# Cos and sin from PSUM, bands in halves, a plain first visit and zero matmuls in a convolution and wave-mixing kernel

## The chip, the cores and the metric

The kernel runs on one core of a Trainium2 chip. The metric is the time of one execution on the device in microseconds (us); of several runs the median is given. A profile is the record of one execution. The engines are named as in the profile: PE is TensorE (matmuls), PEld its weight loads, DVE is VectorE, ACT is ScalarE, POOL is GpSimd and SP is SyncE, which here only issues DMAs.

## The reference

`x` has 8 batches, 4224 tokens and 192 channels. First a causal convolution over 7 tokens runs in each of 8 heads (24 channels each) with softmaxed taps. Its output, again called x, goes through a wave layer. The large part is the mixing over tokens with two 4224 x 4224 matrices.

```python
w = softmax(weight)                       # 8 heads x 7 taps
x = einsum('hk,bskhg->bshg', w, windows_of_7(x))
theta = x @ w_theta                       # 192 x 192
zr, zi = x * cos(theta), x * sin(theta)
y = einsum('ts,bsd->btd', w_tok_r, zr) + einsum('ts,bsd->btd', w_tok_i, zi)
u = x + y
out = u + maximum(u @ w_ch, 0)
```

All inputs and the output are float32. The kernel multiplies in bfloat16 and accumulates in float32.

## The kernel before, in words

**Tiling.** The columns of the token mixing are batch and channel together, 8 x 192 = 1536, split in two halves `g` of 768 (`HN`), each again in two of 384 (`PC`), one PSUM bank per product. Input tokens form 33 chunks of 128, each made of four quarters of 32 tokens from different places of the sequence. Output tokens form 17 units: sixteen pairs of 128-row tiles and a single one. A visit works on one unit with the chunks that are at hand, at most 11 (`SLOTS`). The first visit has chunks 0 and 1, and each of the next nine adds one chunk. Later, chunk c takes the slot of chunk c - 11. After a visit the partial sums of its unit go to DRAM and come back at the unit's next visit.

**Seven products instead of eight.** For a pair of row tiles, the weights of both matrices are a 2 x 2 block A, and the data zr, zi in two halves a 2 x 2 block B. The kernel uses seven products in the manner of Strassen and Winograd (L766 to L846): sums S1 to S4 of the weight blocks (`total`, L576) and T1 to T4 of the data blocks (`sum`, L450). One product costs one 128x384 matmul for each chunk and each half, at L721. With two chunks the first visit has 28 of them.

**A chunk's preparation.** A window loads three quarters of x with halo rows (L277, L293); eight matmuls with the bands, a banded matrix of taps for each head, do the convolution (L323); copies bring the result from PSUM to `xz` (L185 on ScalarE, L183 on VectorE). TensorE transposes it through `ident` (L494), copies bring it to `uT`, and the theta product follows (`channel_mix`, L509). VectorE clamps the angles to +-1.5 on their way from PSUM to the float32 tile `ang` (L397). ScalarE takes cosine and sine of `ang`, 768 columns at a time, into the slot's z tiles r0, i0, r1 (t1 for late chunks) and i1 (L425). VectorE multiplies them by x (L434) and makes the T sums (L446).

**Weights of a visit.** DMAs on POOL's queue load blocks of the two token matrices as bfloat16 into `st` (L542); VectorE transposes them in 32 x 32 blocks (L564) and makes the S sums (L578). Results leave PSUM by adding them into the float32 tiles `d` (L745), or by a plain copy where a unit begins.

**Order.** All steps after the start are planned when the program is built. A `Step` has an engine, a length in us, the steps it follows, and sometimes a bank. `Schedule` walks a model time forward; each engine, when free, takes the ready step with the earliest due time, and the order so found is the order of the instructions on each engine. `START` says when engines and the first data are free. Convolutions, transposes and theta products share banks 6 and 7 (`mm`); the first ones borrow banks 2 to 5 (`lent`). Products use banks 0 to 5: x in 0 and 1, y in 2 and 3, s in 4 and 5. In-order engines mean that an instruction that waits holds up all that stand behind it on its engine.

**The start.** TensorE runs 24 warm-up matmuls on zeros (L963). POOL makes the 0/1 masks with seven selects (L902), a 0/1 `block` with six (L911), and loads `w_theta` (L225). VectorE makes the softmax (L917 to L928), `taps` as a sum of masks (L934), `terms` = taps times weights for all heads (L939), the sum over the 7 taps in three steps (L948) and the three parts of the bands (L953). Before the first visit, two matmuls with `ident` fill the y banks (L781).

Of the kernel before, what the change touches and what calls it, by code (L numbers as in the profile page):

```python
# [16 lines left out]
def kernel(  # L17
# [43 lines left out]
    CLAMP = 1.5  # L61
    EXTRA = 3
    BY_PE = 4
    EITHER, TURNED = 4, 11
# [89 lines left out]
    def parts(u):  # L154
        return 14 if pair(u) else 8
# [58 lines left out]
    nc.vector.memset(bands[:, :, WQ, :], 0.0)  # L214

    def channel_weights(w, name, after=None):
        R = D - P
        made = {}

        def clear():  # L220
            made["t"] = t = wk.tile([P, 4, D], BF16, name=name, tag="wc", bufs=1)
            nc.vector.memset(t[:, 1:3, :], 0.0)

        def load(lo, hi, k, r0, r1):
            pool(nc.gpsimd.dma_start(out=made["t"][lo:hi, k, :], in_=w[r0:r1, :]))  # L225

        pieces = ((0, P, 0, 0, P), (0, R, 1, P, D), (R, P, 2, 0, R), (0, P, 3, R, D))
        if after is None:
            clear()
            for p in pieces:  # L230
                load(*p)
            ready = [Step("none", 0.0, None)]
            ready[0].fixed = START["wth"]
        else:
            ready = [Step("pool", 0.25, lambda: (clear(), load(*pieces[0])), after, lands=4.0, wire=0.3)]
            for p in pieces[1:]:
                ready.append(Step(
                    "pool", 0.6, lambda p=p: load(*p), ready[:1], lands=4.0, wire=0.3
                ))
        return (lambda: made["t"]), ready  # L240

    xw = tiles(wk, 3, [P, B, D], BF16, "xw", bufs=3)
    rings = {k: Ring(2) for k in ("uT", "ang", "xr", "st", "x", "y", "s")}
# [9 lines left out]
    class Window:  # L253
        def __init__(self):
            self.m = len(windows)
            windows.append(self)
            self.k, self.uses, prev = rings["xw"].take()
            self.loads = []
            self.rows = []
            for j in range(WQ):  # L260
                t0, lo = tokens(*divmod(self.m * WQ + j, NQ)), j * ROWS + KS - 1
                s = self.load(lo, t0, Q, prev)
                self.rows.append(s)
                self.loads.append(s)
            for j in range(WQ):
                t0, lo = tokens(*divmod(self.m * WQ + j, NQ)) - KS + 1, j * ROWS
                if t0 < 0:
                    nc.vector.memset(xw[self.k][0 : KS - 1, :, :], 0.0)
                elif self.m < 2:
                    self.loads.append(self.load(lo, t0, KS - 1, prev))  # L270
                else:
                    self.loads.append(self.halo(j, lo, prev))
# [88 lines left out]
    class Chunk:  # L361
# [5 lines left out]
        def prepare(self):  # L367
# [10 lines left out]
            self.ang, angles, anguse, self.z, self.t = {}, {}, {}, {}, {}  # L378
            for g in range(2):
# [6 lines left out]
                ak, anguse[g], prev = rings["ang"].take()  # L386
                self.ang[g] = angt[ak]
                for k2 in range(2):
                    m = Step(
                        "pe", 0.34, lambda b, k2=k2, uT=uT: channel_mix(b, uT, k2, wth()),  # L390
                        [turned, wth_ready, prev], mm=True,
# [4 lines left out]
                    e = Step(  # L396
                        "dve", 0.55, lambda b, k2=k2, g=g: dve(nc.vector.tensor_scalar(  # L397
                            out=self.ang[g][:, k2 * 2 * D : (k2 + 1) * 2 * D],
                            in0=banks[b][:, 0 : 2 * D],
                            scalar1=-CLAMP, scalar2=CLAMP, op0=ALU.max, op1=ALU.min,  # L400
                        )), [m], frees=m,
                    )
                    anguse[g].append(e)
                angles[g] = [s for s in anguse[g]]
            slot = c % SLOTS

            def take(name, key, steps_after, engine, us, run):

                prev = zuses[slot].get(name, [])
                s = Step(engine, us, run, [steps_after, prev])  # L410
                zuses[slot][name] = [s]
                return s

            self.ready = {}
            names = {(0, 0): "r0", (1, 0): "i0", (0, 1): "r1" if self.early else "t1", (1, 1): "i1"}
# [3 lines left out]

            for i, g in ((0, 0), (1, 0), (0, 1), (1, 1)):  # L420
                name = names[i, g]
                self.z[i, g] = z = ztiles[slot][name]

                def wave(z=z, i=i, g=g):
                    act(nc.scalar.activation(  # L425
                        out=z, in_=self.ang[g], func=AT.Sin,
                        **({"bias": half_pi[:], "scale": 1.0} if i == 0 else {}),
                    ))

                w = take(name, None, angles[g], "act", 0.93 if i == 0 else 0.84, wave)  # L430
                anguse[g].append(w)

                def times(z=z, g=g):
                    dve(nc.vector.tensor_tensor(  # L434
                        out=z, in0=self.xf[:, g * HN : (g + 1) * HN], in1=z, op=ALU.mult
                    ))

                s = Step("dve", 0.58, times, [w])
                use(name, s)
                self.xzuse.append(s)  # L440
                self.ready["B" + str(i + 1) + str(g + 1)] = s
            B = self.ready
            self.where = {"B11": "r0", "B21": "i0", "B22": "i1", "T2": "t2", "T4": "t4"}
# [6 lines left out]
            def sum(name, o, p, q, after):  # L450

                if o in (p, q):
                    s = Step("dve", 0.58, minus(o, p, q), after)
                    use(o, s)
                else:
                    s = take(o, None, after, "dve", 0.58, minus(o, p, q))
# [66 lines left out]
    class Weights:  # L523
        def __init__(self, v):
# [70 lines left out]
            turn("A12", "A12")  # L595
            total("S3", "A11", "A21", ALU.subtract, r["A11"] + r["A21"])
# [64 lines left out]
    class Visit:  # L661
# [104 lines left out]
        def products(self):  # L766
# [4 lines left out]
            for r in "xys" if self.pair else "xy":  # L771
                for g in gs:
                    k, uses[r, g], prev[r, g] = rings[r].take()
                    rows[r, g] = 2 * "xys".index(r) + k
                    if self.v == 0 and r != "x":
# [3 lines left out]
                        if r == "y":  # L779
# [32 lines left out]

            for g in gs:
# [34 lines left out]
        def output(self, q):  # L848
            k, use, prev = outring.take()
            if len(outring.uses) <= 5:  # L850
                prev = [
                    s for r in ("ang", "xz", "uT", "xw") for u in rings[r].uses[-3:] for s in u
# [37 lines left out]
    START = {"x": (8.0, 11.0), "pe": 11.3, "dve": 11.3, "act": 6.3, "pool": 11.2, "sp": 2.0, "wth": 15.0}  # L890
# [4 lines left out]
    EARLY, SLACK, CALM = {}, 12.0, 30.0  # L895
    noise = wk.tile([P, 512], BF16, name="noise", tag="ang")
    nc.vector.memset(noise, 0.0)
    Window()
    masks = wk.tile([WR, KS, WQ, Q], BF16, name="masks", tag="ang")
    nc.gpsimd.memset(masks, 1.0)  # L900
    for k in range(KS):
        nc.gpsimd.affine_select(  # L902
            out=masks[:, k, :, :], in_=masks[:, k, :, :], pattern=[[ROWS, WQ], [1, Q]],
            channel_multiplier=-1, base=k, compare_op=ALU.is_equal, fill=0.0,
        )
    Window()
    block = constp.tile([WR, WQ], F32, name="block")
    nc.gpsimd.memset(block, 1.0)
    for j in range(WQ):
        for sign, base in ((1, -j * ROWS), (-1, (j + 1) * ROWS - 1)):  # L910
            nc.gpsimd.affine_select(  # L911
                out=block[:, j : j + 1], in_=block[:, j : j + 1], pattern=[[0, 1]],
                channel_multiplier=sign, base=base, compare_op=ALU.is_ge, fill=0.0,
            )
    wth, wth_ready = channel_weights(moe_w_theta, "wth")
# [6 lines left out]
    nc.scalar.activation(out=wsb, in_=wsb, func=AT.Exp)  # L922
    nc.scalar.activation(out=wmax[:, 0:1], in_=wsb[:, 0, 0:1], func=AT.Sin)
    nc.vector.tensor_reduce(out=wsum, in_=wsb, axis=mybir.AxisListType.X, op=ALU.add)
# [7 lines left out]
    taps = wk.tile([WR, KS, Q], BF16, name="taps", tag="xz", bufs=3)  # L932
    for j in range(1, WQ):
        nc.vector.tensor_tensor(  # L934
            out=taps, in0=masks[:, :, 0, :] if j == 1 else taps, in1=masks[:, :, j, :],
            op=ALU.add,
        )
    terms = spool.tile([WR, KS, H, Q], BF16, name="terms", tag="st")
    nc.vector.tensor_tensor(  # L939
        out=terms, in0=taps[:, :, :].unsqueeze(2).to_broadcast([WR, KS, H, Q]),  # L940
        in1=wbf[0:WR, :, :].rearrange("p h k -> p k h").unsqueeze(3).to_broadcast(
            [WR, KS, H, Q]
        ), op=ALU.mult,
    )
    n = KS
    while n > 1:
        k = n // 2
        nc.vector.tensor_tensor(  # L948
            out=terms[:, 0:k], in0=terms[:, 0:k], in1=terms[:, n - k : n], op=ALU.add
        )  # L950
        n -= k
    for j in range(WQ):
        nc.vector.tensor_scalar_mul(  # L953
            out=bands[:, :, j::NQ, :],
            in0=terms[:, 0].unsqueeze(2).to_broadcast([WR, H, 2, Q]),
            scalar1=block[:, j : j + 1],
        )
    ident = constp.tile([P, P], BF16, name="ident")
    make_identity(nc, ident)

    for k in range(6):
        for _ in range(4):
# [3 lines left out]
    angt = tiles(wk, 2, [P, HN], F32, "ang")  # L966
# [14 lines left out]
    for i, v in enumerate(sequence):  # L981
        for c in entering.get(v, []):
            convolved(c).prepare()
        if v == settled:
# [10 lines left out]
        at += (hi - lo) * parts(u) * (PC / 2400 + 0.0025)  # L995
# [130 lines left out]


# [36 lines left out]
```

## Time and profile before

| | |
|---|---|
| median of 5 runs | 1430.98 us (1426.12 to 1437.35) |
| the profiled execution | 1426.12 us, span 1424.4 us |
| busy: PE, DVE, ACT, POOL | 1398.6, 1100.1, 429.6, 510.3 us |
| mean granted clock of TensorE | 0.993 |
| products at L721 | 7572 matmuls |
| theta and output matmuls at L509, convolution at L323 | 192 columns each; 352 at L323 |
| HBM read, written | 248.53 MB, 104.99 MB |

The span runs from the first instruction to the last. Busy times are those of the profile; matmuls are pipelined, so a busy TensorE is not one at its peak, and counting matmuls in a stretch says more. In rows by group the columns are: line, engine, operation, output<-input with shapes, count, then busy time and the mean of one in ns, then the idle time of the engine just before and what ended it. A row of a timeline begins with the start and the duration in us.

### The profile page before, as it was taken

The page shows a single profiled execution, that of the slowest core. Times are in us where ns is not written, and L with a number is a line of the kernel's source. Part 1 is how long each engine was busy: PE and PEld are TensorE (multiplying, and loading weights), DVE is VectorE, ACT ScalarE, POOL GpSimd, SP SyncE. Part 2 cuts the span into 40 slices and gives each one's busy share as a digit, 9 for nine tenths or more (in the row PEclk, how much of TensorE's full clock was granted, in tenths as well). Part 3 has the DMA queues.
Part 4 walks back from the last instruction along what each step waited for, and adds up shares of the span by engine and source line. Part 5 has one row for each costly group of instructions (what it writes and reads, how often), then busy time and mean ns, then how long its engine had stood idle before and what let it go on. Part 6 is the DMA issues. An engine that isn't in the chain of part 4 may idle for free.

```text
span 1424.4 us, 24789 instructions
## 1 busy us (share of the span) xinstructions
PE 1398.6 (98%) x9318; PEld 884.3 (62%) x9318; DVE 1100.1 (77%) x1803; ACT 429.6 (30%) x761; POOL 510.3 (36%) x779
## 2 busy tenths in 40 slices
PE   6899999999999999999999999999999999999998
PEld 4566666666666666666666666666666666666665
DVE  7998855454887987877657699788897888887787
ACT  5886532212522332320000333234231212111232
POOL 8533321212423464125113445523546153432120
PEclk7999999999999999999999999999999999999999
DMA  8999884567999999999678999999997999999994
GB/s 105 205 228 192 167 161 111 110 116 148 256 207 215 238 232 245 221 216 188 197 166 197 236 223 246 235 238 213 223 220 180 230 257 247 270 238 206 195 257 145
DMA packets 335776, 291.27 MB, mean 204 GB/s; under 512 B 157524, under 2 KB 284500, under 8 KB 335656
## 3 DMA queue, kind: packets, MB, share of 16 engines
q0 software_dynamic: 169232, 97.75, 50.6%
q1 hardware_dynamic: 126424, 182.09, 42.0%
q10 hardware_dynamic: 40000, 9.84, 4.9%
q8 instruction: 73, 1.20, 0.3%
q14 instruction: 47, 0.39, 0.1%
HBM read 248.53 MB, written 104.99 MB: 248 GB/s over the span
## 4 chain that ended last, share of the span: by engine, by line
PE 92%; DVE 3%; issue 1%; DMA 1%; POOL 1%; ACT 1%; SPq 0%; DVEq 0%; POOLq 0%; ACTq 0%
PE bank L721 84%; PE bank L509 5%; PE bank L323 2%; DMA st<-in_moe_w_tok_i_dram 1%; PE bank L494 1%; DVE d L745 1%; DVE w L564 1%; POOL xw L277 1%; DVE d L874 1%; DVE ang L397 0%; ACT xz L185 0%; DVE w L578 0%; DMA xw<-in_x_dram 0%; DVE r L434 0%; ACT r L425 0%
## 5 line engine op out<-in xcount | busy, mean ns | idle before, releaser
L721 PEld LDWEIGHTS <-w 128*128 128x128 bf16 x7572 | 734.8, 98 | 461.3 <-issue 7.9
L721 PE MATMUL bank<-t,w 128*128 128x384 bf16 x3198 | 562.0, 326 | 2.2 <-DVE w L578 0.9
L745 DVE TENSOR_TENSOR d<-bank,d 128x384 f32<-128x384 f32 x532 | 286.9, 547 | 171.7 <-PE bank L721 142.8
L564 DVE STREAM_TRANSPOSE w<-st 128x640 bf16<-128x640 bf16 (+4 forms) x412 | 342.5, 854 | 68.3 <-PE bank L721 55.4
L721 PE MATMUL bank<-r,w 128*128 128x384 bf16 x2154 | 392.1, 326 | 1.4 <-DVE r L434 0.8
L721 PE MATMUL bank<-i,w 128*128 128x384 bf16 x2220 | 389.1, 326 | 1.6 <-DVE bank L183 1.3
L542 POOL DMA_DIRECT2D st<-in_moe_w_tok_r_dram x240 | 137.6, 582 | 400.1 <-DVE w L564 385.6
L542 POOL DMA_DIRECT2D st<-in_moe_w_tok_i_dram x240 | 136.9, 579 | 167.2 <-DVE w L564 150.2
L578 DVE TENSOR_TENSOR w<-w 128x1408 bf16<-128x1408 bf16 (+9 forms) x216 | 182.0, 843 | 2.4
L185 ACT ACTIVATE xz<-bank 32x384 bf16<-32x384 f32 (+2 forms) x300 | 139.7, 481 | 99.3 <-issue 58.4
L277 POOL DMA_DIRECT2D xw<-in_x_dram x137 | 79.1, 584 | 194.5 <-PE bank L323 149.9
L693 POOL TENSOR_TENSOR d<-d,xr 128x768 f32<-128x768 f32 x61 | 103.3, 1695 | 81.6 <-DMA xr<-xs 35.4
L425 ACT ACTIVATE r<-ang,half_pi 128x768 bf16<-128x768 f32 x44 | 41.0, 933 | 285.3 <-DVE ang L397 285.1
L185 ACT ACTIVATE bank<-bank 128x384 f32<-128x384 f32 x111 | 52.3, 474 | 210.6 <-PE bank L721 189.3
L185 ACT ACTIVATE d<-bank 128x384 f32<-128x384 f32 x126 | 60.8, 490 | 137.0 <-PE bank L721 136.2
L397 DVE TENSOR_SCALAR ang<-bank 128x384 f32<-128x384 f32 x132 | 70.7, 552 | 35.9 <-PE bank L509 35.2
L855 ACT ACTIVATE ubT<-d 128x768 bf16<-128x768 f32 x43 | 36.2, 842 | 143.1 <-DVE d L745 131.9
L509 PEld LDWEIGHTS <-uT 128*128 128x128 bf16 x632 | 56.9, 100 | 18.7 <-issue 3.5
L874 DVE SCALAR_TENSOR_TENSOR d<-bank,d 128x384 f32<-128x384 f32 x106 | 54.4, 546 | 12.5 <-PE bank L509 10.8
L509 PE MATMUL bank<-wth,uT 128*128 128x192 bf16 x528 | 62.2, 253 | 0.8 <-ACT uT L185 0.3
L323 PE MATMUL bank<-xw,bands 114*128 114x192 bf16 x352 | 53.2, 252 | 8.3 <-DVE bands L953 4.8
L425 ACT ACTIVATE i<-ang 128x768 bf16<-128x768 f32 x66 | 54.7, 829 | 8.1 <-PE bank L721 8.1
(76 smaller groups left out, 553.9 us busy)
## 6 DMA issues: line engine op xcount, KB each, us to landing
part<-d SPq DMA_DIRECT2D x168, 384.0 KB
d<-part SPq DMA_DIRECT2D x155, 384.0 KB
st<-in_moe_w_tok_r_dram POOLq DMA_DIRECT2D x156, 176.0 KB, 6.2
st<-in_moe_w_tok_i_dram POOLq DMA_DIRECT2D x156, 176.0 KB, 7.1
out_dram<-d SPq DMA_DIRECT2D x53, 384.0 KB
xw<-in_x_dram POOLq DMA_DIRECT2D x132, 96.0 KB, 4.7
xs<-xz SPq DMA_DIRECT2D x132, 96.0 KB
xr<-xs POOLq DMA_DIRECT2D x66, 192.0 KB, 6.3
```

What stands on the lines that cost most here:

```text
L185: act(nc.scalar.activation(out=o(), in_=i(*b), func=AT.Copy))
L277: pool(nc.gpsimd.dma_start(out=xw[self.k][lo : lo + n, :, :], in_=x[:, t0 : t0 + n, :].rearrange("b s d -> s b d"),))
L323: pe(nc.tensor.matmul(banks[b][:, hh * B * G : (hh + 1) * B * G], lhsT=bands[:, h, at : at + NQ, :].rearrange("p z m -> p (z m)"), rhs=xw[ ...
L397: "dve", 0.55, lambda b, k2=k2, g=g: dve(nc.vector.tensor_scalar(out=self.ang[g][:, k2 * 2 * D : (k2 + 1) * 2 * D], in0=banks[b][:, 0 : 2 ...
L425: act(nc.scalar.activation(out=z, in_=self.ang[g], func=AT.Sin, **({"bias": half_pi[:], "scale": 1.0} if i == 0 else {}),))
L509: pe(nc.tensor.matmul(banks[bk][:, b * D : (b + 1) * D], lhsT=tT[:, 3 * k + b + i, :], rhs=w[:, 2 * b + i, :], start=(i == 0), stop=(i == ...
L542: "pool", 0.58, lambda a=a, t0=t0, i=i, w=w: pool(nc.gpsimd.dma_start(out=st[i][a * Q : (a + 1) * Q, 0:nb, 0 : n * Q], in_=w[r0 : r0 + nb ...
L564: lambda c=c, ce=ce: dve(nc.vector.transpose(self.tile(name)[:, c:ce, :, :], st[i][:, at : at + NQ, c * Q : ce * Q].rearrange("p bt (c j) ...
L578: s = Step("dve", 0.15 + 0.069 * n, lambda: dve(nc.vector.tensor_tensor(out=flat(self.tile(name)), in0=flat(self.tile(p)), in1=flat(self.t ...
L693: a = Step("pool", 1.75, lambda: pool(nc.gpsimd.tensor_tensor(out=tile_(), in0=tile_(), in1=xrt[k], op=ALU.add)), [r, s])
L721: pe(nc.tensor.matmul(banks[bank][:, 0:PC], lhsT=self.w.block(a, c), rhs=chunks[c].operand(b, g), start=(start and c == self.lo), stop=(c ...
L745: dve(nc.vector.tensor_tensor(out=o, in0=y, in1=o, op=ALU.add))
```

## The change

- The clamp and the `ang` tiles are gone. ScalarE takes cosine and sine straight from the PSUM bank of the theta product, 384 columns at a time, into the z tile. So the theta product is followed by two ScalarE steps that free its bank, and it now waits for the former users of both z tiles of its half.
- The first visit (`v < PLAIN`, with `PLAIN = 1`) uses eight plain products and needs no S or T sums. Four rings of banks x, y, s and x once more (`z`) take its results, each written out once. The T sums of chunks 0 and 1 are made at visit 1, and the two matmuls at L781 are gone.
- The bands are made in two halves of four heads; one of the three parts of each half is written by ScalarE. The masks come from one select over all taps, on a tile set to one by VectorE; `block` is a maximum over masks on VectorE.
- `w_theta` comes as float32 over SP's queue and is converted by ScalarE. The halo loads of the first two windows stand behind the select and `make_identity`. There are 18 warm-up matmuls. `START` is changed.
- While model time is below `WARM = 60`, the planner emits a 128x128 matmul of zeros wherever its TensorE is free, and counts 0.11 us for it. It adds zeros to columns 384 to 511 of bank 0, which no product uses.

```diff
+            for g in range(2):
...
+                waves = {0: [], 1: []}
+                places = [zuses[slot].get(names[i, g], []) for i in waves]
                 for k2 in range(2):
                     m = Step(
                         "pe", 0.34, lambda b, k2=k2, uT=uT: channel_mix(b, uT, k2, wth()),
-                        [turned, wth_ready, prev], mm=True,
+                        [turned, wth_ready, places], mm=True,
                     )
-                    e = Step(
-                        "dve", 0.55, lambda b, k2=k2, g=g: dve(nc.vector.tensor_scalar(
-                            out=self.ang[g][:, k2 * 2 * D : (k2 + 1) * 2 * D],
-                            in0=banks[b][:, 0 : 2 * D],
-                            scalar1=-CLAMP, scalar2=CLAMP, op0=ALU.max, op1=ALU.min,
-                        )), [m], frees=m,
-                    )
+                    for i in waves:
+                        def wave(b, z=ztiles[slot][names[i, g]], i=i, cols=cols):
+                            act(nc.scalar.activation(
+                                out=z[:, cols], in_=banks[b][:, 0 : 2 * D], func=AT.Sin,
+                                **({"bias": half_pi[:], "scale": 1.0} if i == 0 else {}),
+                            ))
+                        w = Step("act", 0.5, wave, [m], frees=m)
...
+            if v < PLAIN:
+                return
             total("S3", "A11", "A21", ALU.subtract, r["A11"] + r["A21"])
...
+            if self.v < PLAIN:
+                for g in gs:
+                    k, uses["z", g], prev["z", g] = rings["x"].take()
+                    rows["z", g] = k
+                for r, i, j in (("x", 1, 1), ("y", 1, 2), ("s", 2, 1), ("z", 2, 2)):
+                    for g in gs:
+                        product(r, g, f"A{i}1", f"B1{j}", start=True)
+                        product(r, g, f"A{i}2", f"B2{j}")
+                        add(2 * i + j - 3, r, g, begins=True, ends=True)
+                return
...
-    START = {"x": (8.0, 11.0), "pe": 11.3, "dve": 11.3, "act": 6.3, "pool": 11.2, "sp": 2.0, "wth": 15.0}
+    START = {"x": (7.5, 10.5), "pe": 7.5, "dve": 10.5, "act": 8.3, "pool": 8.3, "sp": 4.5, "wth": 9.0}
...
+    for lo, hi, k, r0, r1 in pieces:
+        sp(nc.sync.dma_start(out=wth_f[lo:hi, k, :], in_=moe_w_theta[r0:r1, :]))
     Window()
+    nc.gpsimd.affine_select(
+        out=masks, in_=masks, pattern=[[1, KS], [ROWS, WQ], [1, Q]],
+        channel_multiplier=-1, base=0, compare_op=ALU.is_equal, fill=0.0,
+    )
+    windows[0].halos()
     Window()
+    make_identity(nc, ident)
+    windows[1].halos()
...
+    for hs in (slice(0, H // 2), slice(H // 2, H)):
         nc.vector.tensor_tensor(
+            out=terms[:, :, hs], in0=taps[:, :, :].unsqueeze(2).to_broadcast([WR, KS, H // 2, Q]),
...
+        for j in (1, 0, 2):
+            o = bands[:, hs, j::NQ, :]
+            i = terms[:, 0, hs].unsqueeze(2).to_broadcast([WR, H // 2, 2, Q])
+            if j == 1:
+                nc.scalar.activation(out=o, in_=i, func=AT.Copy, scale=block[:, j : j + 1])
+            else:
+                nc.vector.tensor_scalar_mul(out=o, in0=i, scalar1=block[:, j : j + 1])
...
+        for c in range(NCH):
+            if max(enter[c], PLAIN) == v:
+                chunks[c].sums()
...
+            if now < WARM and self.free["pe"] <= now + 1e-9:
+                self.free["pe"] = now + 0.11
+                if self.emit:
+                    pe(nc.tensor.matmul(
+                        banks[0][:, 3 * P : 4 * P], lhsT=noise[:, 0:P], rhs=noise[:, 0:P],
+                        start=False, stop=True, skip_group_check=True,
+                    ))
```

## Prediction

> **What bounds the kernel now.** I read the page first, then the chain of waits for the price of a steady product, then the busy times by stretch, and last the timeline of the first 45 us.
>
> ```profile
> PE 1398.6 (98%) x9318; PEld 884.3 (62%) x9318; DVE 1100.1 (77%) x1803; ACT 429.6 (30%) x761; POOL 510.3 (36%) x779
> ...
> PEclk7999999999999999999999999999999999999999
> ```
>
> TensorE is busy for 98% of the span and its clock is whole except at the very start. The chain of waits has a stretch with nothing else in it:
>
> ```profile
> 185.82 160.22 PE bank L721 x986
> ```
>
> So a 128x384 product costs 160.22/986 = 0.1625 us. In the same way the timeline's runs at full clock give 0.082 us for a 192-column matmul and 0.056 for a 128-column transpose. With these prices I counted the matmuls in each stretch (groups by shape). From 100 to 1400 us they fill the time: 0.3 us too much or too little in most hundreds, in all about 2 us lost. From 1400 to the end 9.9 us are lost. In the first 100 us 35.9 are lost: 10.0, 7.0, 6.9, 4.4, 3.7, 1.3 in the first six tens, then 1.7 and 0.9 in the two twenties. **So the bulk of what can be won lies before 100 us.** The stretches show who is late there (columns: length, busy time of PE, PEld, DVE, ACT, POOL, clock, DMA share, GB/s):
>
> ```profile
> 10.00:20.00 10.00, 6.04 (x40) 5.18 (x41) 6.94 (x15) 3.61 (x7) 9.99 (x25) 0.58 0.79 100
> 20.00:30.00 10.00, 6.96 (x40) 4.32 (x39) 8.63 (x21) 7.57 (x13) 9.01 (x17) 0.67 1.39 164
> 30.00:40.00 10.00, 7.47 (x48) 4.57 (x47) 9.36 (x19) 8.50 (x15) 2.40 (x5) 0.90 0.42 47
> 40.00:50.00 10.00, 7.93 (x57) 4.58 (x55) 9.64 (x23) 9.07 (x17) 6.26 (x11) 1.00 1.25 237
> 50.00:60.00 10.00, 9.06 (x73) 5.92 (x70) 9.61 (x20) 8.84 (x18) 3.98 (x7) 1.00 1.21 238
> 60.00:80.00 20.00, 19.26 (x134) 11.63 (x133) 18.76 (x38) 17.55 (x35) 10.29 (x18) 1.00 1.20 231
> 80.00:100.00 20.00, 19.44 (x153) 13.06 (x151) 17.44 (x33) 15.35 (x31) 9.44 (x17) 1.00 1.07 209
> ```
>
> From 20 to 80 us VectorE and ScalarE are both full; TensorE waits for them. Before 20 us it waits for the bands, and later for chunk 1:
>
> ```profile
> 13.22 2.74 PE L323 MATMUL bank<-xw,bands 114*128 114x192 bf16 x16 [4.84 <-DVE bands L953]
> ...
> 25.04 0.85 PE L323 MATMUL bank<-xw,bands 114*128 114x192 bf16 x4 [2.06 <-ACT xz L185]
> ...
> 33.48 0.48 PE L721 MATMUL bank<-r,w 128*128 128x384 bf16 x2 [0.85 <-DVE r L434]
> ```
>
> The clock falls twice, at about 11.6 and 25.2 us:
>
> ```profile
> 15.00:18.40 3.40, 2.67 (x21) 2.00 (x19) 2.70 (x5) 2.25 (x6) 3.40 (x7) 0.50 0.96 121
> 18.40:21.80 3.40, 3.07 (x18) 2.36 (x17) 2.61 (x6) 2.01 (x3) 3.34 (x6) 0.50 1.49 165
> 21.80:25.20 3.40, 1.24 (x9) 0.70 (x9) 3.30 (x8) 3.37 (x7) 3.11 (x6) 1.00 1.27 143
> ```
>
> **Bands in two halves, and the start.** In the trace wbf is ready at 5.71, the terms take 2.02 us, their sums 1.35, the three band writes 1.03, and the last band is done at 13.16. Now a maximum over 672 mask columns stands ahead of wbf; 2.02 us for 1792 columns and 0.21 for 56 put it at about 0.85. So wbf comes at 6.7, the first half (1.0 + 0.86 + 0.5) at 9.1 and the second at 11.5. POOL loses two memsets, thirteen selects and four weight loads and gains one long select (seven of 96 columns took 1.63; I put it at 1.0), so its first weight load for the visits goes from 13.49 to about 9.3. The w_theta loads on SP stand ahead of that queue's first other job at 6.26, and hide. But chunk 0 also needs window 1, whose last issue moves only from about 10 to 9.3; with 3.2 us to land (the median) its convolutions can start at 12.5, not at about 14.6. Two cases. If the clock holds, the first product comes at about 18.5 instead of 22.16 (3.7 earlier). If not, the zero matmuls placed between the two windows (the planner thinks window 0 done at 8.4 and window 1 due at 10.7: 2.3/0.11 = 21 of them) run in front of window 1 at half clock, 21 x 0.11 = 2.3 us, and 1.9 are won. I take the middle, **-2.8**.
>
> Here the Trainium skill (TensorE: Matmul & The Clock Gate, Part 1) says that one idle window of some 3.4 us halves the clock and one busy window restores it. The fall at 11.6, 3.2 us after the last warm-up matmul, fits. The return does not: matmuls resumed at 13.22, were 79% busy from 15.0 to 18.4, and the clock came back only at 21.8, after 8.6 us. By the page, a drop in the thin stretch from 7 to 11.6 would be over by about 15; by the row it could last until 22, and of the 2.8 us hardly 1 would stay. The fillers are plain matmuls and close up; I side with the page and keep the row for the range.
>
> **First visit with plain products.** It removes four S sums (0.28 each), and replaces 14 evictions and copies by 8 (0.49 to 0.55 each): 1.1 + 6 x 0.52 = 4.2 us of VectorE and ScalarE work. The eight T sums of chunks 0 and 1 (0.55 each) are moved behind the first visit, not removed. With both engines full, half of the 4.2 is time: **-2.1**. It adds four products, **+0.65**, of TensorE, which is idle there; once TensorE is the bound this counts in full.
>
> **Cos and sin from PSUM.** The relevant rows:
>
> ```profile
> L425 ACT ACTIVATE r<-ang,half_pi 128x768 bf16<-128x768 f32 x44 | 41.0, 933 | 285.3 <-DVE ang L397 285.1
> L185 ACT ACTIVATE bank<-bank 128x384 f32<-128x384 f32 x111 | 52.3, 474 | 210.6 <-PE bank L721 189.3
> L185 ACT ACTIVATE d<-bank 128x384 f32<-128x384 f32 x126 | 60.8, 490 | 137.0 <-PE bank L721 136.2
> L397 DVE TENSOR_SCALAR ang<-bank 128x384 f32<-128x384 f32 x132 | 70.7, 552 | 35.9 <-PE bank L509 35.2
> ```
>
> Each chunk loses four clamps, 2.2 us of VectorE. ScalarE has eight activations of 384 columns instead of four of 768. The nearest row is 0.49 for a sine; the bias adds 0.10 (0.933 against 0.829), so a pair is 1.08 by itself, about 1.0 back to back. Eight then cost 4.0 to 4.4 instead of 3.5: +0.5 to +0.9. Net -1.3 to -1.7 a chunk, and five chunks enter while the two engines are the bound (to about 80 us): 8 us, half of it time, **-4.0**. The other 28 chunks gain nothing: VectorE is hidden behind full TensorE.
>
> What is new is that the theta matmul (L509) now waits for the old users of the z tiles it feeds, and holds its PSUM bank until both waves are done: 1.1 us instead of 0.55. Queued behind it on TensorE are all products. Bounds: 0 where the planner's 0.5 + 0.5 + 0.2 us per pair holds, 0.3 us for each of 132 where ScalarE comes late. Since ScalarE is busy for 58% or less after 100 us and a pair fits 1.2 us, I take 0.
>
> **Zero matmuls.** The second fall of the clock makes chunk 1's transposes and theta matmuls (26.97 to 31.6) run at half speed with ScalarE idle for 2.2 us behind them. At full clock, 16 x 0.08 + 12 x 0.05: **-1.9**. Fillers write spare columns of bank 0. The skill's PSUM page (PSUM — Partial Sum Buffer, Terms) calls two engines in one bank at once an error, so a filler must wait for reads of other columns of bank 0, and TensorE stands behind it. No row shows that wait. In 60 us some 8 reads of that bank occur, 0.55 us each: between 0 and 4.4, and I take **+0.7**, as most fall where TensorE would wait anyway.
>
> Sum: -2.8 - 2.1 + 0.65 - 4.0 - 1.9 + 0.7 = -9.5 us. The profiled execution took 1426.1 (span 1424.4 and 1.7 around it), so 1416.6; the median of the five runs is 1431.0, so 1421.5 there.
>
> **Rivals.**
> - **More comes off (1414):** the savings add up in series, not halved, since each engine waits for the other in the first 45 us. Both engines' 12 us of saved work then count nearly whole: -15 to -17, with 36 lost as the ceiling of about 20 (nothing can multiply before about 18). For it: ScalarE was idle 2.2 us at 28.6 for serial reasons. Against: 96% busy VectorE from 40 us.
> - **The gain is mostly lost (1428):** the fillers, bunched in front of window 1 at half clock and tied to bank 0's readers, eat the earlier start (2.8), the clock stays down (1.9) and the waits at bank 0 cost 2 more; -9.5 + 6.7 = -3. That they don't hold the clock at all is this case, or its milder form.
> - **Slower (1441):** the theta matmul's new waits, at L509. If ScalarE's pair, with what queues ahead of it, takes over the planned 1.2 us, each of 132 stalls TensorE; it decides from 0.13 us a stall (17 us against 9.5 won makes +7.5), and the likely size, 0.15 us, gives 132 x 0.15 - 9.5 = +10. For it: two banks carry all of this traffic. Against: now these 132 waits hold TensorE for under 1 us in all, behind a VectorE that is far busier than ScalarE.
>
> **How the numbers follow.** The likeliest case has 0.50 (0.44 faster, 0.06 within), more 0.22, mostly lost 0.15 (0.14 within, 0.01 slower), slower 0.13. A measurement of this kernel tells about 0.5% (7.2 us) from no change. Range: from 1410, below the second case's 1414, to 1433, past the third's 1428; beyond it lies chiefly the slower case.
>
> **What would show it.** Right: first convolution near 9.1, first product near 18 to 20 and chunk 1's near 28, clock whole from 15 us on, about 26 us lost in the first 100, and every hundred after that full. Wrong: a hundred after 100 us with loss above 1 us waiting on L509's bank; TensorE waiting in a filler for a read of bank 0; a clock below 0.9 between 15 and 30 us; a first product after 21.

## The result and the profile after

The changed kernel takes 1426.14 us (median of 41 runs, 1418.03 to 1438.05) against 1432.26 (78 runs, 1426.12 to 1449.81). The ratio is 0.9954, 95% interval [0.9942, 0.9967]: 6.6 us off, between 4.7 and 8.3. The forecast was 9.5 off, which lies outside that interval; the forecast median, 1421.5, is 4.6 us too low and its range holds the time. (Of the 4.6, 1.3 come from the kernel before, whose median over 78 runs is 1432.3 and not 1431.0.)

The profiled execution of the changed kernel took 1430.14 us (span 1428.4), longer than that of before. That says nothing of the change: before's was the fastest of its 78 runs, this one is 4 us above its median. So I account for each span by its parts, as in the prediction. From the page after:

```profile
PE 1401.9 (98%) x9485; PEld 891.1 (62%) x9485; DVE 1035.9 (73%) x1679; ACT 437.1 (31%) x885; POOL 504.0 (35%) x761
...
PEclk9999999999999999999999999999999999999999
```

VectorE lost 64 us of work, ScalarE gained 7.5, and the clock is whole from the start. The stretches of the changed kernel, with the columns as before:

```profile
10.00:20.00 10.00, 8.50 (x116) 7.63 (x117) 6.28 (x18) 8.42 (x19) 9.50 (x17) 1.00 1.22 138
20.00:30.00 10.00, 9.19 (x93) 6.64 (x92) 7.35 (x16) 8.94 (x20) 5.82 (x11) 1.00 1.23 157
30.00:40.00 10.00, 8.61 (x86) 6.41 (x85) 8.76 (x20) 8.65 (x19) 5.34 (x10) 1.00 0.85 188
40.00:50.00 10.00, 9.63 (x92) 6.85 (x90) 9.31 (x18) 8.21 (x19) 4.92 (x9) 1.00 1.19 239
```

Up to 30 us ScalarE is now the fuller of VectorE and ScalarE. PE's busy time holds the zero matmuls, so again I count. "Loss" is from here on a stretch's length less its real matmuls (zero matmuls and warm-up left out) at the prices of the prediction.

| loss of TensorE, us | 0-20 | 20-40 | 40-60 | 60-100 | 0-100 | 100-800 | 800-1400 | 1400 to end |
|---|---|---|---|---|---|---|---|---|
| before | 17.0 | 11.3 | 5.0 | 2.6 | 35.9 | 0.0 | 3.1 | 9.9 |
| changed | 15.9 | 7.2 | 3.8 | 1.6 | 28.6 | -0.2 | 14.0 | 9.7 |

**The first 100 us lost 7.3 us less; the four added products cost 0.65; that makes 6.7, and 6.6 were measured.** To agree within 0.1 is luck, since such a count repeats within about 1 us (second profiles below) and the measured gain is known to about 2. I take the 11 us more between 800 and 1400 us as a matter of this execution. There TensorE waits, in order, for the transposes of outputs by DMA and for additions into `d`; from 800 to 1400 us the changed kernel shows

```profile
PE bank L501 <- DMA ubT<-ubT: 5.0, 2, 3.9
PE bank L715 <- DVE d L739: 3.4, 2, 2.5
```

(columns: total, times, longest). The longest wait, 3.9 us, is followed by 3.4 us at half clock (1265.9 to 1269.3), in which 16 products took 4.1 us instead of 2.6: a late wait costs more than its own length. A late fall of the clock stands in eight of the fourteen profiles kept here. If the rest of an execution is taken to be as in its profile, the late loss of a mean run can be estimated as that of the profile plus the distance of the mean time from the profiled one: 3.1 + 1433.5 - 1426.1 = 10.4 us before, 14.0 + 1426.7 - 1430.1 = 10.6 after. By this estimate the late part is a scatter of several us between runs, and hardly a difference between the two kernels.

The timeline of the changed kernel around the start:

```profile
10.87 0.93 PE L321 MATMUL bank<-xw,bands 114*128 114x192 bf16 x8 [2.55 <-ACT bands L972]
...
11.63 1.34 PE L1150 MATMUL bank<-noise 128*128 128x128 bf16 x21
...
12.81 0.82 PE L321 MATMUL bank<-xw,bands 114*128 114x192 bf16 x8
...
18.34 0.48 PE L715 MATMUL bank<-r,w 128*128 128x384 bf16 x2
```

The first product moved from 22.16 to 18.34, chunk 1's from 33.48 to 27.04. But the first convolution is at 10.87, not at the forecast 9.1. VectorE's rows say why:

```profile
6.80 2.36 DVE L954 TENSOR_TENSOR terms<-taps,wbf 114x896 bf16<-114x896 bf16 x2
...
9.09 1.28 DVE L963 TENSOR_TENSOR terms<-terms 114x384 bf16<-114x384 bf16 x6
```

The terms of both halves were made first, then all six sums. The program text has them half by half, but these steps lie outside the planner's order (`dve`), and nothing else kept them so. Both halves were ready together, by 11.2.

### The profile page after: what moved, and what is told of

Read it like the earlier page. It is cut to its first block, busy times and chain, and to the rows that moved or that the text cites. A ratio compares the mean times of both kernels' runs of the same rounds, so it can differ in the third digit from the quotient of the medians.

```text
span 1428.4 us, 25083 instructions
## 1 busy us (share of the span) xinstructions
PE 1401.9 (98%) x9485; PEld 891.1 (62%) x9485; DVE 1035.9 (73%) x1679; ACT 437.1 (31%) x885; POOL 504.0 (35%) x761
## 5 line engine op out<-in xcount | busy, mean ns | idle before, releaser
L715 PE MATMUL bank<-r,w 128*128 128x384 bf16 x2162 | 388.1, 326 | 0.3
L570 DVE TENSOR_TENSOR w<-w 128x1408 bf16<-128x1408 bf16 (+8 forms) x212 | 180.5, 852 | 2.6
L184 ACT ACTIVATE xz<-bank 64x384 bf16<-64x384 f32 (+2 forms) x297 | 137.8, 481 | 89.9 <-issue 52.5
L406 ACT ACTIVATE r<-bank,half_pi 128x384 bf16<-128x384 f32 x88 | 47.6, 579 | 264.0 <-PE bank L501 263.8
L501 PEld LDWEIGHTS <-uT 128*128 128x128 bf16 x632 | 54.4, 98 | 12.8 <-issue 1.2
L406 ACT ACTIVATE i<-bank 128x384 bf16<-128x384 f32 x132 | 61.5, 494 | 0.0
L501 PE MATMUL bank<-wth,uT 128*128 128x192 bf16 x528 | 56.9, 246 | 0.3
L501 PE MATMUL bank<-wch,ubT 128*128 128x192 bf16 x424 | 46.2, 247 | 6.2 <-DMA ubT<-ubT 5.0
```

Source lines behind the costliest of these rows:

```text
L184: act(nc.scalar.activation(out=o(), in_=i(*b), func=AT.Copy))
L406: act(nc.scalar.activation(out=z[:, cols], in_=banks[b][:, 0 : 2 * D], func=AT.Sin, **({"bias": half_pi[:], "scale": 1.0} if i == 0 else { ...
L501: pe(nc.tensor.matmul(banks[bk][:, b * D : (b + 1) * D], lhsT=tT[:, 3 * k + b + i, :], rhs=w[:, 2 * b + i, :], start=(i == 0), stop=(i == ...
L570: s = Step("dve", 0.15 + 0.069 * n, lambda: dve(nc.vector.tensor_tensor(out=flat(self.tile(name)), in0=flat(self.tile(p)), in1=flat(self.t ...
L715: pe(nc.tensor.matmul(banks[bank][:, 0:PC], lhsT=self.w.block(a, c), rhs=chunks[c].operand(b, g), start=(start and c == self.lo), stop=(c ...
```

## The experiments

Ratios are to the kernel before, with 95% intervals; "later than the changed kernel" is the difference of two ratios times 1432 us. From the two intervals, such a difference is uncertain by an estimated 3 us for the kernels with 22 runs, and by 4 to 5 us for those with 11 to 14; a loss comes from one profile and repeats within about 1 us. The first four kernels undo or alter one thing in the changed kernel.

**Without zero matmuls.**

```diff
-    EARLY, SLACK, CALM, WARM = {}, 12.0, 30.0, 60.0
+    EARLY, SLACK, CALM, WARM = {}, 12.0, 30.0, 0.0
```

> The changed kernel without the zero matmuls. My theory (the clock falls again in the thin stretches near 12 and 25 us, and that costs more than the fillers' own waits at bank 0): loss of TensorE in the first 100 us rises from 28.6 us to about 30 to 31, the clock of a stretch between 10 and 30 us is 0.5 to 0.8, ratio to the kernel before 0.996 to 0.998. Rival (the zero matmuls are ballast: what they save in clock they cost in waits at bank 0, 1.9 us in the profile): loss 27.5 to 28.6, ratio 0.994 to 0.9955.

Loss in the first 100 us 28.4, ratio 0.998 [0.9961, 1.0], which is 3.7 us later than the changed kernel. The two theories each got one half: the ratio is the theory's, the loss the rival's. The clock did fall, to 0.83 in the mean of both 10 to 20 and 20 to 30 us, for 3.4 us each time. Still the loss there is no larger. One reason is that the 21 zero matmuls no longer stand between the two windows:

```profile
10.89 2.36 PE L321 MATMUL bank<-xw,bands 114*128 114x192 bf16 x16 [2.33 <-ACT bands L972]
```

All sixteen convolutions run in one go and the first product comes at 18.07, a little sooner than at 18.34. So in the first 100 us of these profiles the zero matmuls cost what they save. Where the 3.7 us are, this profile doesn't show; it is of the second fastest of the 22 runs.

**Seven products in the first visit.**

```diff
-    EITHER, TURNED, PLAIN = 4, 11, 1
+    EITHER, TURNED, PLAIN = 4, 11, 0
```

> The changed kernel with seven products in the first visit again (S sums, T sums and the bank fill come back, four products less). My theory (4.2 us of work on VectorE and ScalarE shared by two full engines, less the four products): 1.5 us slower than the changed kernel, loss in the first 100 us about 30.7 of which four products are 0.65, ratio to before 0.9965. Rival (the sums are only moved to the second visit and the engines catch up later): within 0.5 us of the changed kernel, loss 28.6 to 29.3. Another rival (the first visit's chain is serial and the saving counts whole): 4 us, loss 33.

Loss 30.2, ratio 0.9953 [0.9934, 0.9973]. Less the 0.65 us of the four products that are gone again, that is 1.0 us more in the first 100 us; by the ratios it is 0.1 us less. The plain first visit is worth about 1 us by the count, and the ratios can't tell that from 0 or from the forecast 1.45.

**The clamp and the angle tiles back.**

```diff
+                    clamps.append(Step(
+                        "dve", 0.55, lambda b, k2=k2, ang=ang: dve(nc.vector.tensor_scalar(
...
+                    w = Step("act", 0.93 if i == 0 else 0.84, wave, [clamps, places[i]])
```

> The changed kernel with the clamp and the float32 angle tiles back. My theory (1.3 to 1.7 us of net work per chunk on two full engines, five chunks): 4 us slower than the changed kernel, loss in the first 100 us about 32.6, ratio to before 0.998. Rival (the first three chunks alone count, as TensorE's losses after 50 us are small in both): 1.5 to 2.5 us, loss 30 to 31. Rival of the other sign (the longer hold of the bank cost time that now comes back): loss 28.6 or less.

Loss 32.8, ratio 0.9986 [0.9956, 1.0015]: 4.2 us by the loss and 4.6 by the ratio, as my theory had it. In this profile the clock also fell once, from 12.2 to 15.6; the loss up to 20 us has only some 0.5 of the 4.2.

**The halves of the bands one after the other.** All steps from the terms to the bands, and the two ScalarE steps ahead of them, are put into the order of the text.

```diff
-        nc.vector.tensor_tensor(
+        dve(nc.vector.tensor_tensor(
             out=terms[:, :, hs], in0=taps[:, :, :].unsqueeze(2).to_broadcast([WR, KS, H // 2, Q]),
...
```

> The changed kernel with the two halves of the bands forced to come one after the other on VectorE and ScalarE; in the changed kernel VectorE made the terms of both halves first, so that the bands were ready at 10.3 to 11.2. My theory (window 1 and not the bands sets the end of chunk 0): first convolution at about 9.0 instead of 10.9, first product at 18.0 to 18.4 as now (18.3), loss in 100 us within 0.5 of 28.6. Rival (the bands are the chain): first product near 17, loss near 27.

Loss 31.8, ratio 0.9965 [0.9946, 0.9985]: 3.2 us later by the loss, 1.6 by the ratios. Neither theory held. The first convolutions come at 10.39, but then:

```profile
12.93 0.80 PE L321 MATMUL bank<-xw,bands 114*128 114x192 bf16 x4 [2.05 <-ACT bands L972]
13.52 2.45 PE L1150 MATMUL bank<-noise 128*128 128x128 bf16 x21
15.76 0.95 PE L321 MATMUL bank<-xw,bands 114*128 114x192 bf16 x8
```

The second half comes later than in the changed kernel, TensorE is busy for 0.5 us of the 3.4 before 12.6, the clock halves there, and the 21 zero matmuls run at half clock (2.45 us instead of 1.34) in front of window 1. The first product is at 21.43. This is the second of the two cases in the prediction's start (fillers at half clock in front of window 1), and worse than it: 0.7 us are won there instead of 1.9. It came with the very order that the prediction assumed.

The next two take one part by itself; the third takes one out of the change.

**Cos and sin from PSUM alone, in the kernel before** (the same edit as in the change, with the waits for the z tiles; it starts from the kernel before).

> The kernel before with one part of the change alone: cosine and sine straight from PSUM, no clamp. The undo of this part cost 4.6 us in the mean. My theory (shared vector work of five chunks, whatever the clock does): 4 us faster than before, ratio 0.997, loss in the first 100 us about 32, mean clock still near 0.992. Rival (it pays only with a whole clock): 0 to 1.5 us, ratio 0.999 to 1.0. Rival of the other sign (theta products that wait at their bank): slower, with TensorE waiting at L509 after 100 us.

Ratio 0.9968 [0.994, 0.9996], 4.6 us faster (0.6 to 8.6); mean clock 0.9919 as before (0.9912 beside it). The loss in its profile is 33.9, only 2.0 less. So the timing sides with my theory, the loss lies nearer to the rival, and whether the clock matters for the size is not settled. Two things in the profile speak for a smaller gain by itself. In the first 100 us the clock stood at half for 20.5 us, against 17.1 in both profiles of the kernel before. And theta matmuls waited in the first 100 us for the sine that frees their bank:

```profile
PE bank L493 <- ACT i L407: 2.1, 4, 1.1
```

The prediction put this wait at 0; the changed kernel without zero matmuls has 1.8 us of it, and in the kernel before the clamp brought 1.0. After 100 us it is gone, other than behind output steps.

**The zero matmuls alone, in the kernel before** (the added lines of the change; the tile of zeros lies in another buffer).

> The kernel before with the zero matmuls alone. Without them the changed kernel spent 19 us at half clock in the mean of its runs instead of 5, and took 4.0 us longer. My theory (every us at half clock that is removed in the first 60 us is worth about 0.3 us, in either kernel): mean clock 0.996 to 0.998 instead of 0.992, 4 us faster than before, ratio 0.997. Rival (what my prediction said): 1.2 us, ratio 0.999. Rival (waits at bank 0 in an order that was not planned from a right start time eat it): 0 or slower.

Ratio 0.9975 [0.9943, 1.0007], mean clock 0.9964 instead of 0.9912; loss 35.2, 0.7 less. The clock came as I said. Between 4 and 1.2 us, or 0, the interval doesn't choose; the loss in the first 100 us is nearest to the lower ones.

**The changed kernel with the old start.**

```diff
-    START = {"x": (7.5, 10.5), "pe": 7.5, "dve": 10.5, "act": 8.3, "pool": 8.3, "sp": 4.5, "wth": 9.0}
+    START = {"x": (8.0, 11.0), "pe": 11.3, "dve": 11.3, "act": 6.3, "pool": 11.2, "sp": 2.0, "wth": 15.0}
```

(with the old masks, block, bands, 24 warm-up matmuls, and loads of `w_theta` on POOL)

> The changed kernel with the start of before: bands in one piece, masks and weights on POOL, old start times in the planner. My theory (the start is worth what the first product's time says, 3.8 us, less what the engines behind are late anyway): first product near 22 instead of 18.3, loss in the first 100 us 31 to 32, 2.5 us slower than the changed kernel, ratio 0.997. Rival (the whole 3.8): ratio 0.998. Rival (later work absorbs it): ratio 0.9955, loss within 1 of 28.6.

First product 20.63, sooner than I said: the clock fell at 12.8 and was back at 16.2, against 21.8 before. Loss 31.8, ratio 0.997 [0.9935, 1.0004]: 3.2 us by the loss, 2.3 by the ratios. My theory fits in size.

**True start times in the planner.**

```diff
-    START = {"x": (7.5, 10.5), "pe": 7.5, "dve": 10.5, "act": 8.3, "pool": 8.3, "sp": 4.5, "wth": 9.0}
+    START = {"x": (10.6, 10.8), "pe": 7.5, "dve": 11.2, "act": 11.0, "pool": 8.3, "sp": 4.5, "wth": 9.0}
```

> The changed kernel with start times in the planner as the profile has them (x at 10.6 and 10.8, VectorE 11.2, ScalarE 11.0), so that the 21 zero matmuls between the convolutions of window 0 and window 1 stand ahead of both. My theory (these fillers, 1.3 us at whole clock, held window 1 up; its data were there, as without zero matmuls both windows were convolved in one go from 10.9): first product about 1 us earlier than 18.3, clock whole to 30 us, loss in 100 us 27.6, ratio to before 0.9945. Rival (transposes and the engines behind set the pace): first product within 0.3 of 18.3, loss 28.6, ratio 0.9955. Rival (another plan with other waits): loss over 29.5.

```profile
7.50 1.84 PE L1150 MATMUL bank<-noise 128*128 128x128 bf16 x30
10.87 0.93 PE L321 MATMUL bank<-xw,bands 114*128 114x192 bf16 x8 [1.53 <-ACT bands L972]
...
17.75 0.48 PE L715 MATMUL bank<-r,w 128*128 128x384 bf16 x2
```

Thirty zero matmuls now fill the gap before the bands, and five stand between the windows. The first product is 0.6 us sooner, the loss 27.5, the clock whole. Ratio 0.9945 [0.9917, 0.9973], median 1423.16: the fastest of all kernels here, 7.9 us off before, though its interval holds the changed kernel too.

**Later landings in the planner.** The run beside it is the one above.

```diff
-        "x": 9.0, "halo": 5.5, "keep": 6.0, "turn": 11.0, "w": 8.0, "d": 7.5, "store": 5.5,
+        "x": 9.0, "halo": 5.5, "keep": 6.0, "turn": 17.0, "w": 8.0, "d": 10.0, "store": 5.5,
```

> The same, and in the planner an output's transpose by DMA is taken to land after 17 us instead of 11, a partial sum after 10 instead of 7.5. Theory (the 7 to 14 us lost between 800 and 1400 us are TensorE waiting in order for late DMAs, and most of the scatter between runs is that): loss from 800 to 1400 us 2 to 5 us, 4 to 6 us faster than the run beside it, ratio 0.991. Rival (the loads are late because the DMA engines are full, and waiting elsewhere replaces it): loss 7 to 14 as now, no gain; or the tail after 1400 us grows by up to 5 us.

Slower: 1.0022 [1.0001, 1.0044], loss from 800 to 1400 us 17.0. The waits for DMA transposes are gone, and 6.2 us of waits for evictions into `late`, the tile of a partial sum, and 3.2 for the data of an entering chunk have come. My theory fell: the waiting moves, as the rival said. That the DMA engines are full, the rival's reason, is not shown by this.

**Zero matmuls up to 30 us only.**

```diff
-    EARLY, SLACK, CALM, WARM = {}, 12.0, 30.0, 60.0
+    EARLY, SLACK, CALM, WARM = {}, 12.0, 30.0, 30.0
```

> The changed kernel with zero matmuls only up to 30 us of the plan instead of 60. Theory (the two falls of the clock lie before 30 us, later fillers only add waits at bank 0): as fast as the changed kernel or up to 1 us faster, mean clock 0.997 or more. Rival (TensorE is thin enough up to 60 us for the clock to fall there too): 1 to 3 us slower, mean clock 0.995.

Ratio 0.9983 [0.9954, 1.0012], mean clock 0.9969, loss 29.3 in the first 100 us, and 25.1 from 800 to 1400, of which 9.4 are waits for DMA transposes. Neither theory in full: from 30 to 60 us the clock stayed whole and the loss (4.8) is below that of the changed kernel (7.1), as the theory had it, but the time is the rival's. The early clock is not the reason for that: it fell at 13.0, as it did in other kernels with zero matmuls, and was back at 16.4. It is slow late.

**Second profiles.** Two kernels as they were.

> A second profile of the changed kernel without zero matmuls. The first profiled execution had a mean clock of 0.997, the best of its 22 runs (mean 0.9934). My theory (how long the clock stays at half depends on where the fall meets the work, and a usual execution loses more in the first 100 us than the 28.4 of that profile): mean clock 0.993 to 0.995, loss in the first 100 us 30 to 33. Rival (the clock costs nothing in the first 100 us, the 4 us come from late waits for DMA): loss 28 to 29 whatever the clock, loss from 800 to 1400 us over 12.

> A second profile of the kernel before. The profiled execution was the fastest of 78 runs, 6 us below their median. Theory: loss in the first 100 us again near 36 (35 to 38), loss from 800 to 1400 us 6 to 12 instead of 3.1. Rival (the first 100 us scatter as much as the late part): a loss there of over 39.

The kernel without zero matmuls: 1433.13 us, clock 0.995, loss 28.9 in the first 100 us and 16.5 from 800 to 1400. The rival holds: its clock was at half for 10.2 us in the first 100, against 6.8 in the first profile, and the loss is only 0.5 larger. The kernel before: 36.8 and 3.8. So the first 100 us repeat within 1 us and the late part does not, though 3.8 is below the 6 to 12 that I expected.

## Why the prediction was right, and where it was not

**The place** was right: in the profiles all that was won lies before 100 us, and "28 other chunks gain nothing" held.

**Cos and sin, -4.0:** right beside the other parts. Undone, it costs 4.2 (loss) or 4.6 us (timing); by itself it brought 2.0 (loss) or 4.6 (timing). The rows are

```profile
L406 ACT ACTIVATE r<-bank,half_pi 128x384 bf16<-128x384 f32 x88 | 47.6, 579 | 264.0 <-PE bank L501 263.8
...
L406 ACT ACTIVATE i<-bank 128x384 bf16<-128x384 f32 x132 | 61.5, 494 | 0.0
...
L501 PE MATMUL bank<-wth,uT 128*128 128x192 bf16 x528 | 56.9, 246 | 0.3
```

A pair takes 1.07 us, forecast 1.08. TensorE stood idle 0.3 us ahead of all 528 theta matmuls: the slower case has no ground. The bank's longer hold was not free everywhere, though: in the two kernels with this part and no zero matmuls it shows as waits of 2.1 and 1.8 us (for the clamp it was 1.0 before), all in the first 100 us, where the prediction took 0.

**Start, -2.8:** right in size (3.2 by the loss, 2.3 by the timing), wrong in the way. "The first half at 9.1" failed, because nothing held the halves apart. Held apart, they made the start worse: the second half was later, and the zero matmuls planned between the windows ran at half clock. The size was partly luck: of the two cases the whole clock came in the profile, and the clock's fall near 13 us, which would have brought the other, stands in five of the nine kernels with zero matmuls.

**First visit, -2.1 + 0.65:** probably too large, but within what can be told. The profile gives 1.0 net, the timing 0, where 1.45 were forecast. What speaks against "with both engines full, half of the 4.2 is time": in the changed kernel VectorE is 63 to 74% busy from 10 to 30 us, so it is not full where the work was taken away (ScalarE is 84 to 89% busy), and the sums that moved to the second visit fall where VectorE is 88 to 93% busy (30 to 50 us).

**Zero matmuls, -1.9 + 0.7:** in the first 100 us this term came to 0; by the timing, with its uncertainty of 3 us, they are worth 3.7. The clock was held as forecast, whole from the start, so "clock whole from 15 us on" is right. What failed is the reckoning of what that saves and costs. The saving was read from the kernel before, whose second fall lasts 6.8 us (25.2 to 32.0); with the other parts of the change in place and no zero matmuls it lasts 3.4 (24.2 to 27.6). And there are two costs: 1.34 us of zero matmuls in front of window 1 (in the prediction this was reckoned only for a halved clock; with most of them moved ahead of both windows, under true start times, the loss was 1.1 lower), and the waits at bank 0, which TensorE's list of waits in the first 100 us shows:

```profile
PE bank L1150 <- DVE bank L182: 1.3, 2, 0.7
```

With another 0.6 behind an eviction to `d` that is up to 1.9 us where I took 0.7, within the bounds of 0 to 4.4; a wait costs its whole length only if real work stood ready behind it. Removing the zero matmuls leaves the loss at 28.4 to 28.9.

**The sum.** Forecast were 4.0 + 2.8 + 1.45 + 1.2, or 9.5. Undone one at a time, the parts cost 4.2, 3.2, 1.0 and 0, in all 8.4 us of loss, and together they brought 6.7. So about 1.1 of the missing 2.8 us lie in single terms, chiefly the zero matmuls, and about 1.7 in the step that added the terms as if they were independent. They are not: cosine and sine from PSUM are worth 4.2 us beside the other parts and 2.0 alone. Each of these figures has about 1 us of scatter, so the split is an estimate.

**What stays open.** Without zero matmuls the kernel is 3.7 us slower by the timing, yet its two profiles show no more loss than the changed kernel's in the first 100 us. Its mean time leaves an estimate of 14 to 15 us of late loss instead of 10.6, and its two profiles have 7.3 and 16.5, with the instructions of VectorE in the same order in both. The planner, whose TensorE is then free at other times, puts the later instructions into another order than in the changed kernel. Whether the order, the clock or chance makes it slow late is not settled. The profile with zero matmuls up to 30 us is slow late too (25.1), so I don't count the 3.7 us for the zero matmuls themselves; it isn't shown that they aren't worth them.

**On the clock rule.** In the changed kernel there was no fall to test in the first 100 us; the kernel without zero matmuls has one:

```profile
10.50:13.90 3.40, 2.23 (x17) 1.34 (x17) 2.27 (x7) 3.30 (x9) 3.40 (x7) 1.00 1.01 76
13.90:17.30 3.40, 3.39 (x25) 3.01 (x26) 1.80 (x5) 2.65 (x5) 3.40 (x7) 0.51 1.40 210
17.30:20.70 3.40, 2.23 (x15) 1.28 (x14) 2.62 (x5) 3.06 (x8) 2.85 (x6) 0.99 1.36 179
```

The clock fell at about 14.0 and was back at 17.3, after one stretch of 3.4 us in which PE was all but full. That is what the Trainium skill says (TensorE: Matmul & The Clock Gate, Part 1): one busy window restores it. The prediction's row is no exception to that, if a stretch that is 79% busy doesn't count as busy. In the fourteen profiles, the end of the kernel left out, the clock stays at half for 3.4, 6.8 or 10.2 us, that is for one, two or three such stretches. It came back after 25 stretches with 2.9 to 3.4 us of PE (85% and more), and stayed down after 12 with 1.2 to 2.9. So for these traces the line between the two lies near 85%. In the kernel before it lasted 10.2 us from 11.6 on, since the first two stretches had 1.8 and 2.7 us. Where it fell at 12 to 14 us with zero matmuls (five kernels), the stretch had 2.9 to 3.4 us and the clock was back after 3.4. So siding with the page was right for work that is filled up in this way.

## What to carry to other kernels

Count real matmuls at their steady price in every stretch, and compare stretches, when two single profiles differ by less than the runs scatter: here the slower profile belonged to the faster kernel. Work added to an idle engine that runs in order is not free where its place comes from a planned time; zero matmuls belong ahead of the wait that is known to be long. A bank that nobody reads should spare them the waits seen here; no run tried it. A part that moves work saves only what the engine that gets it has to spare.

## What the runs showed of the hardware

- A stretch does not have to be idle for the clock to fall, and its busy time alone doesn't decide it: before, 1.24 us of PE in the 3.4 us from 21.8 to 25.2 were followed by a fall, and 1.81 in those from 32.1 to 35.5 were not; without zero matmuls 2.23 us from 10.5 to 13.9 were followed by one and 2.23 from 17.3 to 20.7 were not.
- The same kernel meets these falls at other times in another execution: before, at 11.6 and 25.2 us in one profile, at 14.1, 24.4 and 34.6 in the second.
- Zero matmuls of 128 columns take 0.056 us each at whole clock (the last start of 21 within 1.34 us, less one latency of 0.22) and 0.107 at half (13.52 to 15.76). 65, 36, 26, 28 and 12 of them in the five tens from 10 to 60 us went with a whole clock in the changed kernel. In all nine profiles with zero matmuls there is no fall from 17 to 100 us, and in all five without them there is; but five of the nine still have one fall at 12 to 14.
- One select over 672 columns on POOL took 0.94 us, seven of 96 columns 1.63.
- In this kernel a matmul into unused columns of a bank waited for copies out of that bank's other columns: 1.9 us in 60.
